# Attention, a mixture of experts and a dense layer in one kernel: GpSimd instead of SyncE issues some loads between the experts

## The chip, the cores and the metric

The kernel runs on one core of a Trainium2 chip. The metric is the device time of one execution, in microseconds (us); a kernel's time is the median of its runs. Queues: SP is SyncE's instruction stream, POOL is GpSimd's, and both issue DMAs; PE is TensorE, DVE VectorE, ACT ScalarE.

## What is computed

```
x = causal_attention(q, k, v)            # 4 x 12 heads, 448 positions, 64 wide: 1792 tokens x 768
e = argmax(x @ w_gate)                   # one of 8 experts for each token
y = gate * relu(x[e] @ w1[e]) @ w2[e]    # w1: 8 x 768 x 1024, w2: 8 x 1024 x 768
h = y @ w_in                             # 768 x 2048
out = (h - tanh(h)) @ w_out              # 2048 x 768
```

Inputs and output are float32. The kernel splits each float32 operand into a high and a low float16 part and multiplies three of the four combinations.

## The kernel before, in words

There are three stages: attention with the routing (0 to about 235 us in the profile), the experts (to about 535 us), and the last stage with the dense layer (to the end). The change touches the experts, which are run one after the other.

**A slot** (`slot`, L872) is 128 tokens of one expert. Expert e has one first slot, which always runs, and then as many further slots as its token count asks for; these stand in nested branches (`extra`, L945: `tc.If` at L949, taken or skipped on a count that all engines hold in a register). In the profiled run the experts 1 to 6 take 2, 3, 1, 2, 1 and 5 slots. PE does in a slot 144 matmuls of the first product (`mm1_f`, L164), then 12 transposes of token rows for a later slot (`planes_T`, L151), then 48 matmuls of the second product in two halves (`mm2_k`, L176), in the first slot with 12 more transposes between the halves. ACT and DVE take the first product out of PSUM with the relu (`slot_relu`, L171 and L172; tiles hh and hl), and PE's second product waits for these.

**Raw loads and pieces.** The weights come from DRAM as float32 into two buffers, raw1 for w1 and raw2 for w2 (the profile calls both raw), 14 pieces in all: six of w1 (512 KB each) and eight of w2 (384 KB). While the first slot of expert e runs, ACT writes the high part of each piece of expert e+1 (L115) and DVE the low part (L123, in `pieces`), and behind that the freed place is loaded with the piece of expert e+2 (`load_raw`, L107). The slot calls `fill_lo` at four places, z = 0 to 3, with 1, 4, 4 and 5 pieces (`PLAN`, L1031). The calls z = 0 to 2 stand before the slot's result is stored (`ys_d`, L923), and the one with the last five pieces, all of w2, behind that store. All 14 loads are issued by SP, in this order, and each waits for DVE's low part of its piece.

**Other traffic.** Each further slot also converts two or three units of the dense layer's weights (`conv_fill`, L1001): a unit of 1 MB is loaded into one of the buffers cu (`conv_load`, L990, SP), DVE and ACT turn it into float16 planes (L980 to L986, L115, L123; tiles cc and co), and the planes are stored (`conv_store`, L1007, SP). A unit's load waits for DVE to have read the unit before it in that buffer. GpSimd fetches token rows by index (`slot_rows`, L861, tiles xg and xg_n), each behind the transposes that read the rows before, and does some elementwise work. In expert 6's first slot, behind its store, SP loads the first six row blocks of the last stage (`prep0`, L1071; 384 KB each) from ys_d into the raw buffers, which are free by then; they wait for all stores to ys_d so far.

**Branches.** A branch that is skipped has a path of its own, in which the semaphores are brought to where the taken path would leave them. On SP these paths wait for the DMAs that SP has in flight on the named semaphores.

Of the kernel before, what the change touches and what calls it, by code (L numbers as in the profile page):

```python
# [19 lines left out]
AX = mybir.AxisListType  # L20
PSUM = bass.MemoryType.PSUM
SP = mybir.EngineType.SP

B, H, S, D = 4, 12, 448, 64
CP, NCH = 112, 4
# [30 lines left out]
GS = [sum(GB[:i]) for i in range(len(GB))]  # L56
# [3 lines left out]
def build(ctx: ExitStack, tc: tile.TileContext, kq0, kq, v, wg, wo, w1, w2, wf, out):  # L60
    nc = tc.nc
# [27 lines left out]
    flg = cst.tile([1, 5], I32, name="flg")  # L89
# [5 lines left out]
    raw1 = raw_p.tile([128, KD, F1], F32, name="raw1")  # L95
    raw2 = raw_p.tile([128, KF1, DM], F32, name="raw2")
# [6 lines left out]
    mctl = tc.manual_schedule()  # L103
    mctl.__enter__()

    def load_raw(e, x, k, n=1):
        nc.sync.dma_start(out=(raw1, raw2)[x][:, k : k + n, :], in_=(w1, w2)[x][e, :, k : k + n, :])  # L107

    def w_tiles(e, zs=(0, 1)):
        return [w16s[e % 2][z].tile((([128, 2, KD, F1]), [128, 2, KF1, DM])[z], F16, tag=f"w{z + 1}", name=f"w{z + 1}_{e}")  # L110
# [23 lines left out]
        for x, k, eh, el in plan:  # L134
            scaled(eh, w[x][:, 0, k, :], (raw1, raw2)[x][:, k, :])

    def pieces(w, plan, nxt=None, hi=True):
        if hi:
            pieces_hi(w, plan)
        for x, k, eh, el in plan:  # L140
            rest_of(el, w[x][:, 1, k, :], (raw1, raw2)[x][:, k, :], w[x][:, 0, k, :])
        if nxt is not None and nxt < E:
            for x, k, eh, el in plan:
                load_raw(nxt, x, k)

    def planes_T(rows, hi, lo, pool, tag="t", eng="a"):
        for x, dst in enumerate((hi, lo)):
# [786 lines left out]
    ystores = {}  # L934

    def after(ins, names):
        for n in names:
            tc.add_manual_dep(ins, n, mybir.DependencyInfo(mybir.DependencyClass.Sync, mybir.DependencyReason.DATA),
                              reason="reads or overwrites what these stores wrote")
# [125 lines left out]
    yq_of = lambda g, i: first["yq"][g][i] if g < 2 else G["yq"]  # L1065
    dg_of = lambda g, i: first["dg"][g][i] if g < 2 else dgs[i % 2]

    def prep0(g, i, r0=None, to=None):
        bk = GS[g] + i
        src = ys_d[bk * 128 : (bk + 1) * 128] if r0 is None else ys_d[ds(r0, 128)]  # L1070
        after(nc.sync.dma_start(out=yg_of(g, i) if to is None else to, in_=src).ins, sum(ystores.values(), []))  # L1071

    def prep_s(g, i, n):
        b0 = GS[g] + i
# [128 lines left out]
    wts = {0: wts0, 1: wts1 + w_tiles(1, (1,))}  # L1203
# [24 lines left out]
    for e in range(E):  # L1228
        if e == 0:
            slot_rows(0, 2, 1)  # L1230
            slot_rows(1, 0, "n")
        slot_rows(e, 2 + FB[e], 0)
        if e == 0:
            next(tl, None)
        if e + 1 < E:
            if e:
                wts[e + 1] = w_tiles(e + 1)

            def fill_hi(z, e=e):
                todo = PLANS[e]  # L1240
                if e:
                    pieces_hi(wts[e + 1], sum(todo, [])[CUT[z] : CUT[z + 1]])
                else:
                    pieces_hi(wts[e + 1], todo[max(z - 1, 0)] if z != 1 else [])

            def fill_lo(z, e=e):
                if e == 0 and z >= 2:
                    next(tl, None)
                pieces(wts[e + 1], PLANS[e][z], e + 2, False)
                if e == 1 and z == 3:  # L1250
                    order_b()
                if e == E - 2 and z == 3:
                    early = nc.values_load(flg[0:1, 4:5], engines=(SP,), min_val=0, max_val=128)
                    for g in range(2):
                        for i in range(GB[g]):
                            prep0(g, i, early * (GS[g] + i) if g + i else 0)

            fill = (fill_hi, fill_lo)
        else:
            wo_ = [w16s[0][z].tile([128, KF2, DM], F16, tag=tg, name=f"wo_{z}") for z, tg in enumerate(("w1", "w2"))]  # L1260
            wof = [t.rearrange("p k f -> p (k f)") for t in wo_]
            stg = [wof[0][:, z * 4096 : (z + 1) * 4096].bitcast(U32).rearrange("p (n t) -> p n t", t=2) for z in range(2)]
            stg += [wof[1][:, z * 2048 : (z + 1) * 2048] for z in range(2)]
            planes_ = [[wof[1][:, 2048 + z * row : 2048 + (z + 1) * row] for z in range(3)],
                       c3[2:4] + [wof[1][:, 6656 : 6656 + row]]]
            first["yq"] = [[t.rearrange("p (k x n) -> p k x n", k=KD, x=2) for t in ts] for ts in planes_]
            first["dg"] = [[wof[1][:, 8192 + 768 * g + 256 * z : 8448 + 768 * g + 256 * z].bitcast(BF16).rearrange(
                "p (a n) -> p a n", a=2) for z in range(3)] for g in range(2)]
            first["sc"] = [wof[1][:, 9728 + 64 * g : 9792 + 64 * g].bitcast(F32) for g in range(2)]
            second = nc.values_load(flg[0:1, 0:1], engines=(SP,), min_val=0, max_val=128)  # L1270
            remaining()
            qc = (cc, wof[0][:, 8192:10240].bitcast(U32))

            def fill(z):
                if z == 2:
                    first_hi()
                if z in (1, 2):
                    to_f32([(qc[2 - z][:, h], cu[z - 1][:, h, :]) for h in HS])
                    conv_planes(qc[2 - z], co[z - 1][:, 0], co[z - 1][:, 1], "p")
                    conv_store(z - 1, nc.values_load(flg[0:1, z + 1 : z + 2], engines=(SP,), min_val=0, max_val=NDY - 1))  # L1280
                if z == 1:
                    for q in range(2):
                        conv_load(stg[q], NDY + q, nc.gpsimd)
                    prep_max(0, 0, GB[0])
                    first_planes()
                if z == 3:
                    prep_max(1, 0, GB[1])

            qhl = [[y[:, (10 + q) * 1024 : (11 + q) * 1024] for y in wof] for q in range(2)]

            def last_f32(q):
                to_f32([(qc[q][:, h], stg[q][:, h, :]) for h in HS])

            def last_planes(q):
                for z in range(2):
                    for h in HS:
                        c = qc[q][:, h].bitcast(F32)
                        scaled("a", qhl[q][0][:, h], c) if z == 0 else rest_of("p", qhl[q][1][:, h], c, qhl[q][0][:, h])

            def last_fill(z):  # L1300
                if z == 1:
                    last_f32(0)
                    first_rest()
                if z == 2:
                    last_planes(0)

        slot(e, FB[e], wts[e], f"n{e % 2}", fill,
             ((1, (FB[e] + 1) % 2),) + ((("n", f"n{(e + 1) % 2}"),) if e + 1 < E else ()),
             [lambda j=j: slot_rows(*j) for j in ((e + 1, 1, 1), (e + 2, 0, "n")) if j[0] < E], late=e + 1 == E, mid=lambda: counts(e))
        if e == 0:  # L1310
            for _ in tl:
                pass
            sctx.close()
            cv = w16ctx.enter_context(tc.tile_pool(reuse_waits="tile", name="cv", bufs=1, side="right"))
            cu = [cv.tile([128, 1024, 2], U32, name=f"cu_{z}") for z in range(2)]
            cc = cv.tile([128, 1024], U32, name="cc")
            co = [cv.tile([128, 2, 1024], F16, name=f"co_{z}") for z in range(2)]
            cuf = [t.rearrange("p n t -> p (n t)").bitcast(F16) for t in cu]
            cof = [t.rearrange("p a n -> p (a n)") for t in co]
            ccf = cc.bitcast(F32)  # L1320
            ny = KD * 384
            spare = [t[:, ny:4096].bitcast(F32) for t in cuf]
            yg1 = cof[1][:, 0 : 2 * DM].bitcast(F32)
            dgs = [cof[1][:, 1536 + 256 * z : 1792 + 256 * z].bitcast(BF16).rearrange("p (a n) -> p a n", a=2) for z in range(2)]
            rss = [cof[0][:, 768 * z : 768 * (z + 1)].bitcast(BF16).rearrange("p (a n) -> p a n", a=2) for z in range(2)]
            sc = [cof[0][:, 1536 + 64 * z : 1600 + 64 * z].bitcast(F32) for z in range(2)]
            G = {0: {"yh": cuf[0][:, 0:ny].rearrange("p (k n) -> p k n", k=KD),
                     "yl": cuf[1][:, 0:ny].rearrange("p (k n) -> p k n", k=KD), "rs": rss[0]}}
            oba = cof[1][:CP, 0 : NC_ * 128].bitcast(BF16).rearrange("p (c n) -> p c n", n=128)
            ob = ccf[:CP, 0 : 3 * NC_ * NBLK].bitcast(BF16)  # L1330
            obm = ob[:, 0 : NC_ * NBLK].rearrange("p (c n) -> p c n", c=NC_)
            obb = ob[:, NC_ * NBLK :].rearrange("p (c n z) -> p c n z", c=NC_, z=5)
            for z in range(3):
                order_a(z)
            conv_load(cu[0], 0)
        if e == E - 1:
            wi_load(nc.sync, 0)
        extra(e, 1 + FB[e], wts[e])
        if e == 0:
            conv_load(cu[1], unit_of(1, 1))  # L1340
# [200 lines left out]
```

## Time and profile before

| | |
|---|---|
| median of 3 runs | 1000.73 us (996.85 to 1002.29) |
| profiled execution | 998.19 us, of which the span of the trace is 996.5 us |
| PE busy | 956.4 us of the span |
| DVE, ACT, POOL busy | 788.6, 613.8, 471.7 us |
| DMA queue of SP / of GpSimd | 144.68 MB / 19.80 MB |

The profiled execution is 2.54 us below the median. A busy time of an engine is a sum over its instructions; an idle time before an instruction is put down to what came last of what it waited for. DMA-issuing instructions on SP are shown where SP issues them (SPq); on POOL a DMA's span is the time that GpSimd works on issuing it. "To landing" is from issue to the last byte.

### The profile page before, as it was taken

To read this page: it belongs to the slowest core of one execution; us is meant where nothing else is said; L and a number is where in the kernel's file an instruction comes from. 1 tells how busy PE (TensorE), PEld (TensorE's weight loads), DVE (VectorE), ACT (ScalarE), POOL (GpSimd) and SP (SyncE) were. 2 spreads that over 40 slices of the span, in tenths; PEclk is the share of its full clock that TensorE was granted. 3 is DMA by queue.
4 is the path that set the end of the run, shared out by engine and by line. 5 is a ranking of instruction groups with operands and counts; after the bars stand their busy time and mean duration, and the time that the engine had idled before them with its cause. 6 is when DMAs were issued, how large, how long until landed. Compare 5 with 4: busy or idle time off the path is not lost. (4 is left out here: it accounts for less than half of the span.)

```text
span 996.5 us, 24098 instructions
## 1 busy us (share of the span) xinstructions
PE 956.4 (96%) x9177; PEld 714.8 (72%) x9177; DVE 788.6 (79%) x1740; ACT 613.8 (62%) x1176; POOL 471.7 (47%) x536
## 2 busy tenths in 40 slices
PE   5999999998999999998999899999999999999996
PEld 4998989986787878787686556666666666677764
DVE  7878888978879598797888999887988788786630
ACT  5898988763645484753356896656565556565530
POOL 7668887872211020202246797555544434443321
PEclk9999999999999999999999999999999999999999
DMA  9787786576799999979876430010000000000000
GB/s 253 213 234 212 217 230 181 164 258 239 274 399 335 345 344 344 345 266 327 305 289 233 171 152 17 32 33 17 24 25 32 17 25 17 9 17 17 16 25 24
DMA packets 59703, 166.36 MB, mean 167 GB/s; under 512 B 7904, under 2 KB 21856, under 8 KB 56480
## 3 DMA queue, kind: packets, MB, share of 16 engines
q1 hardware_dynamic: 54992, 144.68, 43.1%
q0 software_dynamic: 4560, 19.80, 5.8%
q8 instruction: 80, 1.31, 0.5%
q14 instruction: 71, 0.58, 0.2%
HBM read 122.21 MB, written 29.62 MB: 152 GB/s over the span
## 5 line engine op out<-in xcount | busy, mean ns | idle before, releaser
L1430 PE MATMUL fo<-wo,g 128*128 128x384 f16 x1344 | 228.2, 326 | 0.0
L1379 PEld LDWEIGHTS <-raw 128*128 128x128 f16 x1440 | 140.7, 98 | 85.2 <-issue 6.9
L1430 PEld LDWEIGHTS <-g 128*128 128x128 f16 x1344 | 131.2, 98 | 83.8
L1389 POOL TENSOR_TENSOR V<-cu,cc 128x384 f32<-128x384 f32 (+1 forms) x80 | 79.2, 990 | 185.6 <-ACT cu L1388 184.5
L164 PEld LDWEIGHTS <-w 128*128 128x128 f16 x2592 | 145.8, 98 | 7.7 <-issue 6.6
L1379 PE MATMUL fh<-cu,raw 128*128 128x384 f16 (+1 forms) x864 | 131.8, 308 | 3.3 <-DVE cc L1387 3.3
L378 ACT ACTIVATE P<-s,nb 112x112 f32<-112x112 f32 (+1 forms) x192 | 91.4, 509 | 23.6 <-DVE nb L370 21.6
L123 DVE SCALAR_TENSOR_TENSOR w<-raw,w 128x768 f16<-128x768 f32 (+1 forms) x99 | 99.7, 1067 | 0.2 <-ACT w L115 0.2
L861 POOL DMA_INDIRECT xg<-xs_d,idx x22 | 26.9, 1221 | 150.8 <-PEq L949 29.2
L1388 ACT ACTIVATE cu<-cc 128x384 f32<-128x384 f32 (+1 forms) x80 | 40.0, 500 | 92.5 <-DVE cc L1387 92.5
L115 ACT ACTIVATE w<-raw 128x768 f16<-128x768 f32 (+2 forms) x106 | 90.0, 909 | 9.8 <-DMA raw<-w 5.5
L370 DVE CUSTOM_DVE_ANT_0 s<-s,maskw 112x112 f32<-112x112 f32 (+1 forms) x192 | 86.1, 455 | 9.5 <-PE s L364 4.6
L1387 DVE TENSOR_TENSOR cc<-fh,co 128x384 f32<-128x384 f32 (+1 forms) x80 | 42.0, 525 | 63.2 <-PE fh L1379 50.2
L1392 POOL TENSOR_TENSOR X<-cc,X 128x384 f32<-128x384 f32 (+1 forms) x80 | 88.2, 1102 | 4.1 <-ACT X L1391 0.5
L427 PE MATMUL o<-v,PT 112*112 112x65 f32 x576 | 83.8, 269 | 0.0
L1399 DVE SCALAR_TENSOR_TENSOR V<-cu,V 128x384 f32<-128x384 f32 (+1 forms) x80 | 82.2, 1028 | 0.2
L1407 DVE TENSOR_TENSOR V<-V,co 128x384 f32<-128x384 f32 (+1 forms) x64 | 78.3, 1224 | 0.0
L1408 ACT ACTIVATE g<-V 128x384 f16<-128x384 f32 (+1 forms) x80 | 40.0, 500 | 46.4 <-DVE V L1407 46.3
L1379 PE MATMUL fh<-yh,raw 128*128 128x384 f16 x384 | 67.6, 326 | 0.7 <-DVE cc L1387 0.7
L397 PE MATMUL t<-ident,P 112*112 112x112 f32 x480 | 68.0, 265 | 0.0
L427 PEld LDWEIGHTS o<-v,PT 112*112 112x112 f32 x576 | 67.8, 177 | 0.0
L363 PE MATMUL s<-kh,qa 128*112 128x112 f16 (+1 forms) x192 | 53.8, 302 | 11.4 <-POOL qa L298 7.3
(677 smaller groups left out, 2093.9 us busy)
## 6 DMA issues: line engine op xcount, KB each, us to landing
raw<-w SPq DMA_DIRECT2D x48, 512.0 KB, 7.3
raw<-w SPq DMA_DIRECT2D x64, 384.0 KB, 9.4
cu<-wf SPq DMA_DIRECT2D x22, 1024.0 KB, 8.2
wb_d<-co SPq DMA_DIRECT2D x22, 512.0 KB, 8.1
raw<-kq SPq DMA_DIRECT2D x11, 896.0 KB, 6.9
raw<-wb_d SPq DMA_DIRECT2D x8, 768.0 KB, 4.6
raw<-v SPq DMA_DIRECT2D x12, 448.0 KB, 7.5
xs_d<-xq SPq DMA_DIRECT2D x24, 224.0 KB, 2.5
```

What stands on the lines that cost most here:

```text
L115: nc.scalar.activation(out=out, in_=in_, func=AF.Copy, scale=WS)
L123: nc.vector.scalar_tensor_tensor(out=out, in0=in_, scalar=WS, in1=hi, op0=ALU.mult, op1=ALU.subtract)
L164: nc.tensor.matmul(out=ph[:, (f % 4) * 128 : (f % 4 + 1) * 128], lhsT=w[0][:, ww, k, f * 128 : (f + 1) * 128], rhs=xTs[tag][:, xx, k, :], ...
L370: nc.vector.tensor_tensor_reduce(out=d["s", m][:, z, :], in0=d["s", m][:, z, :], in1=maskw[:, S - n : S], scale=-0.125, scalar=3.0e38, op0 ...
L378: nc.scalar.activation(out=d["P"][:, j, OFF[i] : OFF[i] + n], in_=d["s", m][:, z, :], func=AF.Exp, bias=d["nb"][:, 2 * i + j : 2 * i + j + ...
L427: nc.tensor.matmul(out=po[:, i, :], lhsT=d["PT"][:, PT_AT[g], o : o + CP], rhs=d["t"][3][:, hl, j, :], start=(j == 0), stop=(j == i))
L1379: nc.tensor.matmul(out=ph[:, 0:nt], lhsT=wi[ww][:, f // 4, k, f % 4 * 128 : (f % 4 + 1) * 128], rhs=yy[:, k, 0:nt], start=(q == 0), stop=( ...
L1389: nc.gpsimd.tensor_tensor(out=d["V"], in0=d["U"], in1=d["h"], op=ALU.mult)
L1392: nc.gpsimd.tensor_tensor(out=d["X"], in0=d["h"], in1=d["X"], op=ALU.subtract)
L1399: nc.vector.scalar_tensor_tensor(out=d["V"], in0=d[f"S{z}"], scalar=QD[z - 1], in1=d["V"], op0=ALU.add, op1=ALU.mult)
L1407: nc.vector.tensor_tensor(out=d["V"], in0=d["V"], in1=rs_y(g, nt), op=ALU.mult)
L1430: nc.tensor.matmul(out=po[:, 0:384], lhsT=t[:, x, k, i * 128 : (i + 1) * 128], rhs=wo_[ww][:, k, z * 384 : (z + 1) * 384], start=(k == 0 a ...
```

## The change

`load_raw` and `prep0` get a parameter for the issuing engine. From expert 1 on, the loads behind the last five pieces (z = 3) are issued by GpSimd; so are the six row loads in expert 6's first slot, with the register that holds their stride (`early`), which is now loaded on POOL. What is loaded, where to, and what each load waits for on DVE stay.

```diff
-    def load_raw(e, x, k, n=1):
-        nc.sync.dma_start(out=(raw1, raw2)[x][:, k : k + n, :], in_=(w1, w2)[x][e, :, k : k + n, :])
+    def load_raw(e, x, k, n=1, eng=nc.sync):
+        eng.dma_start(out=(raw1, raw2)[x][:, k : k + n, :], in_=(w1, w2)[x][e, :, k : k + n, :])
...
-    def pieces(w, plan, nxt=None, hi=True):
+    def pieces(w, plan, nxt=None, hi=True, eng=nc.sync):
...
-                load_raw(nxt, x, k)
+                load_raw(nxt, x, k, 1, eng)
...
-    def prep0(g, i, r0=None, to=None):
+    def prep0(g, i, r0=None, to=None, eng=nc.sync):
...
-        after(nc.sync.dma_start(out=yg_of(g, i) if to is None else to, in_=src).ins, sum(ystores.values(), []))
+        after(eng.dma_start(out=yg_of(g, i) if to is None else to, in_=src).ins, sum(ystores.values(), []))
...
-                pieces(wts[e + 1], PLANS[e][z], e + 2, False)
+                pieces(wts[e + 1], PLANS[e][z], e + 2, False, nc.gpsimd if e and z == 3 else nc.sync)
...
-                    early = nc.values_load(flg[0:1, 4:5], engines=(SP,), min_val=0, max_val=128)
+                    early = nc.values_load(flg[0:1, 4:5], engines=(POOL,), min_val=0, max_val=128)
...
-                            prep0(g, i, early * (GS[g] + i) if g + i else 0)
+                            prep0(g, i, early * (GS[g] + i) if g + i else 0, None, nc.gpsimd)
```

In the order of instructions only SP and POOL differ. On SP behind expert 5's first slot (the store of its result, then the branch to its further slots), before:

```order
L923 ISA
L923 DMA ys_d<-yo_I-14133_14134 128x768
L107 DMA raw_90<-w 128x768 x5
L949 COMPARE_AND_BRANCH
L944 REGISTER_ALU
L1537 BRANCH_PREFETCH_HINT
```

and now:

```order
L924 ISA
L924 DMA ys_d<-yo_I-14133_14134 128x768
L950 COMPARE_AND_BRANCH
L945 REGISTER_ALU
L1538 BRANCH_PREFETCH_HINT
```

The five loads have left SP; they stand on POOL, in expert 5's first slot behind the fetch of xg_n. With the semaphores that each row waits for (DMASW are those of GpSimd's own DMAs, used in turn), before:

```order
L861 DMA xg_n<-xs_d,idx 128x1536 [waits DMASW6_49,PE_49]
L949 COMPARE_AND_BRANCH
L944 REGISTER_ALU
L1537 BRANCH_PREFETCH_HINT
L861 DMA xg_4588<-xs_d,idx 128x1536 [waits DMASW2_49,PE_49]
```

now, with the fetches at expert 6's beginning as the last two rows:

```order
L862 DMA xg_n<-xs_d,idx 128x1536 [waits DMASW0_49,PE_49]
L108 DMA raw_90<-w 128x768 [waits DMASW1_49,DVE_49]
L108 DMA raw_90<-w 128x768 [waits DMASW2_49,DVE_49]
L108 DMA raw_90<-w 128x768 [waits DVE_49] x3
L950 COMPARE_AND_BRANCH
...
L862 DMA xg_4588<-xs_d,idx 128x1536 [waits DMASW6_49,DMASW1_49,DMASW7_49,DMASW0_49,PE_49]
L862 DMA xg_4589<-xs_d,idx 128x1536 [waits DMASW2_49,PE_49]
```

All of the next expert's fetches now stand behind the five loads, and the first of them waits for the semaphore DMASW1, which the first of the five uses.

On SP behind expert 6's first slot, before (of the six row loads three are left out here):

```order
L923 DMA ys_d<-yo_I-16037_16038 128x768
L1253 TENSOR_LOAD flg
L1253 ISA x2
L1071 DMA raw_89<-ys_d 128x768
L1071 ISA
L1071 DMA raw_89<-ys_d 128x768
...
L1071 DMA raw_90<-ys_d 128x768
L949 COMPARE_AND_BRANCH
...
L990 DMA cu_4987<-wf 128x2048
```

and now:

```order
L924 DMA ys_d<-yo_I-16037_16038 128x768
L950 COMPARE_AND_BRANCH
L945 REGISTER_ALU
L1538 BRANCH_PREFETCH_HINT
L1017 TENSOR_LOAD xtab
L1017 ISA x2
L991 ISA
L991 DMA cu_4987<-wf 128x2048
```

SP comes from the store straight to the unit's load; the six row loads stand on POOL, ahead of the fetch of token rows in expert 6's first further slot.

## Rows read from the trace of the kernel before

**Rows 1.** The head of the page.

```profile
span 996.5 us, 24098 instructions
```

**Rows 2.** Windows: stretch, length, busy PE, PEld, DVE, ACT, POOL, clock, DMA share, GB/s.

```profile
250.00:430.00 180.00, 177.09 (x2189) 142.28 (x2188) 146.56 (x212) 104.95 (x149) 28.23 (x22) 1.00 0.93 342
450.00:530.00 80.00, 75.37 (x899) 59.16 (x897) 67.07 (x122) 31.50 (x58) 28.23 (x30) 1.00 0.84 298
```

**Rows 3.** Waits of PE, 250 to 530 us: us in total, times, longest.

```profile
PE py_I-16959_16960 L176 <- ACT hh_I-16750_16751 L171: 2.2, 1, 2.2
PE py_I-17308_17309 L176 <- ACT hh_I-17100_17101 L171: 0.9, 1, 0.9
PE py_I-16221_16222 L176 <- ACT hh_I-16033_16034 L171: 0.8, 1, 0.8
PE py_I-16959_16960 L176 <- DVE hl_I-16752_16753 L172: 0.2, 1, 0.2
```

**Rows 4.** Timeline of SP, 395 to 440 us: start, length, instruction.

```profile
395.96 0.59 SPq L1007 DMA_DIRECT2D wb_d<-co  x1
408.94 6.61 SPq L107 DMA_DIRECT2D raw<-w  x9
417.97 0.36 SPq L923 DMA_DIRECT2D ys_d<-yo_I-14133_14134  x1
419.17 5.75 SPq L107 DMA_DIRECT2D raw<-w  x5
435.07 0.35 SPq L923 DMA_DIRECT2D ys_d<-yo_I-16037_16038  x1
438.32 3.54 SPq L1071 DMA_DIRECT2D raw<-ys_d  x6
442.94 0.33 SPq L990 DMA_DIRECT2D cu<-wf  x1
```

**Rows 5.** Waits of SP, 395 to 412 us.

```profile
SPq L949 <- SPq L949: 11.6, 5, 5.1
```

**Rows 6.** Timeline of DVE, 400 to 460 us; in brackets idle time before, and what ended it.

```profile
406.11 0.55 DVE L119 TENSOR_SCALAR w<-raw 128x768 f16<-128x768 f32 x1
...
407.05 8.16 DVE L123 SCALAR_TENSOR_TENSOR w<-raw,w 128x1024 f16<-128x1024 f32 x9
439.76 1.28 DVE L986 SCALAR_TENSOR_TENSOR cc<-cu,cc 128x512 uint32<-128x512 uint32 x2
451.06 0.76 DVE L980 TENSOR_SCALAR cc<-cu 128x512 uint32<-128x512 uint32 x2 [4.16 <-DMA cu<-wf]
```

**Rows 7.** Timeline of ACT, 415 to 456 us.

```profile
417.85 1.06 ACT L115 ACTIVATE w<-raw 128x1024 f16<-128x1024 f32 x1 [1.87 <-DMA raw<-w]
453.71 1.24 ACT L115 ACTIVATE co<-cc 128x512 f16<-128x512 f32 x2 [7.15 <-DVE cc L986]
```

**Rows 8.** Timeline of POOL, 400 to 440 us.

```profile
405.35 1.66 POOL L861 DMA_INDIRECT xg_n<-xs_d,idx  x1 [3.63 <-PE pt_I-14416_14417 L151]
409.34 1.48 POOL L861 DMA_INDIRECT xg<-xs_d,idx  x1 [2.33 <-PEq L949]
437.09 0.94 POOL L861 DMA_INDIRECT xg<-xs_d,idx  x1 [17.88 <-PE pt_I-16567_16568 L151]
```

**Rows 9.** GpSimd's issues, by line: least, median and greatest ns; then their landing.

```profile
L990 POOL DMA_DIRECT2D wo<-wf x2: 577/604/631, 515.9 to 516.5; - x2
L861 POOL DMA_INDIRECT xg<-xs_d,idx x22: 940/942/3551, 234.9 to 510.0; - x22
DMA to landing us min/median/max: 3.6/7.1/11.0
```

**Rows 10.** DMAs cu<-wf, SP's line L990: least, median and greatest us to landing.

```profile
DMA to landing us min/median/max: 5.5/8.2/12.1
```

**Rows 11.** Timeline of PE: the transposes of fetched rows in expert 6's first two further slots.

```profile
435.98 0.50 PE L151 MATMUL pt_I-16558_16559<-identh,xg 128*128 128x128 f16 x6
452.49 0.50 PE L151 MATMUL pt_I-16908_16909<-identh,xg 128*128 128x128 f16 x6
```

More of the change, by code (lines that the diff above doesn't have):

```diff
@@ L22 @@
 SP = mybir.EngineType.SP
+POOL = mybir.EngineType.Pool
 B, H, S, D = 4, 12, 448, 64
```

## The prediction

> **What bounds the kernel now.** I start from the head of the page for the span, 996.5 us [rows 1], and then ask what PE waits for where the change acts, between 250 and 530 us. The windows say that PE is busy for 177.09 of the 180 us up to 430, and for 75.37 of the 80 us from 450 on [rows 2]: this stage is PE's, and whatever any queue does earlier or later is worth only what it takes from PE's idle 2.9 and 4.6 us, or adds to them. The waits of PE name the parts that a load can reach [rows 3]: 0.8 us in expert 6's first slot and 2.2 + 0.2 us in its third (its second further slot), both for the relu of ACT and DVE (hh, hl), and 0.9 us in its fourth. A part of the rest is the fetch of code at branches, which no load changes.
>
> Next, what makes the relu late. In expert 6's first slot ACT, which works in order, stands for 1.87 us before a high part, for a raw load [rows 7]; the relu comes behind it. In the third slot ACT stands for 7.15 us behind DVE's conversion [rows 7], and DVE for 4.16 us, until 451.06, for a unit's load [rows 6].
>
> Then SP's timeline, for why those loads are late [rows 4]. The unit's load is issued at 442.94. DVE had read the unit before it by 441.04 (439.76 + 1.28) [rows 6]; in between SP was busy with the six row loads, 438.32 to 441.86, which wait for the store of 435.07 to land. And behind expert 4's last store (395.96) SP issues nothing until 408.94: 11.6 us of that are waits of the skipped branches for SP's own DMAs [rows 5]. Then come nine raw loads, the slot's store at 417.97, and the last five from 419.17 on. DVE was done with all their pieces at 415.21 (407.05 + 8.16) [rows 6].
>
> **The change, part by part.** The sum is made against the profiled execution, 998.19 us, which lies 2.54 below the median of 1000.73.
>
> *Twenty-five raw loads leave SP* (five each in experts 1 to 5). On POOL they no longer stand behind the store, so each can go when DVE has finished its piece: in expert 5 the last at about 415 instead of 424. Each is needed one first slot later, so being earlier is worth nothing by itself. What counts is that SP has fewer DMAs to wait for in the skipped branches and that less is queued ahead of its own, so that the raw load which ACT misses by 1.87 us comes earlier. With that PE's 0.8 us goes. I take -0.8; bounds 0 (the transfers share the same engines, and only their order changes) and -1.0 (the 0.2 us of DVE behind it as well).
>
> *The six row loads leave SP.* The unit's load goes at about 441.1 instead of 442.94: 1.8 us earlier. That alone leaves 4.16 - 1.8 = 2.4 us of DVE's wait and 2.4 - 1.8 = 0.6 us of PE's. Besides, the load no longer queues behind 2.4 MB of rows in SP's queue. Before, it landed 8.1 us after its issue; the least of the 22 such loads is 5.5 [rows 10], so up to 2.6 us more. I take -2.2, near the upper bound of -2.4 (the whole stall), because the rows and the unit now sit in two queues and the unit no longer has to let all rows pass; the lower bound is 0. The Trainium skill, DMA: Bandwidth & Descriptors, section "Issuing engines are not separate DMA queues", says that DMAs issued by several engines interleave on the same 16 DMA engines and that this saves only the issuing time. By that rule the term would be the 1.8 us alone.
>
> *Expert 6's later slots* keep their waits, which come from units issued as soon as DVE lets them: 0, with bounds of 0 and -1.3 (0.9, and some 0.4 for DVE's parts).
>
> *What GpSimd has to do for it.* The nearest row is the only plain DMA it issues today, 577 to 631 ns [rows 9]; a fetch by index takes 942 ns in the middle, 3.55 us once [rows 9]. I take 0.6 us. 25 x 0.6 + 6 x 0.6 = 18.6 us of POOL, of which nothing lies on the path by itself: in this stage POOL is busy for 28 of 180 us [rows 2]. What counts is who stands behind them:
> - The five loads: behind them is the next expert's first fetch, which by the order now also waits for the first of the five to land. In expert 5 that is at about 411.6 + 8.2 = 420 (0.9 us of DVE for each piece, 8.2 us to landing as a unit's load has it [rows 10]) instead of 409.34 [rows 8]. The rows then land at about 420.6 + 7.1 = 428 [rows 9], by the greatest landing at 432. PE transposes them at 435.98 [rows 11]. Cost 0, cover 4 to 8 us; in expert 3, the other case without a further slot, the same distance.
> - The six row loads: POOL waits as SP did until 438.32, then 6 x 0.7 us (0.6 and the register work between) to 442.5. The fetch behind them leaves at 442.5 instead of 437.09 [rows 8] and lands 7.1 us later at 449.6, at worst 11.0 later at 453.5. PE transposes these rows at 452.49 [rows 11]. Cost 0; bounds 0 and +1.0 (453.5 - 452.49), or +2.8 if the loads take 1 us each and the landing is the worst one. This is the thinnest cover of all.
>
> Sum: -0.8 - 2.2 + 0 + 0 = **-3.0 us**: 995.2 for the profiled execution, and from the median 1000.73 - 3.0 = **997.7 us**. What PE gains in this stage is passed on to the end, since in the last stage PE and DVE follow on each other without a fixed date.
>
> **Rivals.**
> 1. *Nothing to see* (within 1 us of before, some 1000.7). The unit's load and the rows move the same bytes over the same engines, so the unit may land at 451 all the same, and what the first slot gains is lost again at the third slot's transposes. For it: DMA runs at 0.93 of its share up to 430 and 0.84 after [rows 2]. Against it: the queue is idle just before 438, so the unit's load is held back by issue and order there, not by a backlog.
> 2. *Slower: GpSimd's issuing becomes the wait.* Place: the fetch behind the six row loads. It has to leave by 452.49 - 7.1 = 445.4, so the loads may take (445.4 - 438.3) / 6 = 1.2 us each. A fetch of xg_n took 1.66 us at 405.35 instead of 0.94 [rows 8, 9]; one fetch took 3.55. With 1.66 each: 438.3 + 10.0 + 7.1 = 455.4, 2.9 us after 452.49, which replaces the 2.4 us of before: about 1000.4 with the first slot's gain. With 3.55 each: 438.3 + 21.3 + 7.1 = 466.7, a stall of 14.2 instead of 2.4, so 1000.7 - 0.8 + 11.8 = 1011.7. It decides from about 2.5 us each on. The Trainium skill, SBUF — State Buffer, section "SBUF: two separate sides", says that GpSimd cannot write a DMA's descriptors while DVE runs an instruction in a mode that takes the port they share. The trace agrees for the issue at 405.35, during which DVE scales a piece (L119, 406.11 [rows 6]). Against the rival: at the moved loads DVE mostly runs other lines (L123, L983), and the middle of the fetches beside those is 942 ns [rows 9]; only two short L980 fall on the six.
> 3. *All waits for loads go* (0.8 + 0.2 + 2.2 + 0.2 + 0.9 + 0.4 = 4.7 us): 996.0. For it: DVE and ACT come through the third slot earlier, and each later slot inherits that. Against: the 0.9 us hangs on a unit that is issued without delay already.
> 4. *The loads do not come earlier*, if POOL is held up by its fetches ahead of them: then only the second term is left, 998.5. The order speaks against it: the fetch before the five is done in the middle of the slot, at 407.0 in expert 5 [rows 8].
>
> **How the numbers follow.** Chances: forecast, with rival 4 as its weaker form, 0.52; rival 1 0.25; rival 2 0.10; rival 3 0.13. A measurement tells 0.5% (5 us: below 995.7 or above 1005.7) from no change. The forecast lies 2.0 above that line and the three runs of before lie 5.4 apart, so a sixth of its chance falls below (0.09); rival 3 lies at 996.0, so nearly half does (0.06); with 0.02 for the rest, faster is 0.17. Slower is rival 2 where its loads take over 2.5 us (0.07) and 0.02 of stray: 0.09. Same is 0.74. The range reaches down to rival 3 less 3 us of scatter, 993.0, and up to no change plus 2.8, half of the runs' scatter or the cost of a late fetch: 1003.5.
>
> **What would show it.** Right: on SP the unit's load of expert 6's second slot at 441 to 442 and no loads behind the stores; DVE's wait of 4.16 us under 2 us; the wait of PE for hh in the third slot under 0.5 us, that in the first slot gone; on POOL the five loads before the store, 0.6 us each; the fetch behind the six at about 443, landed before PE's transposes. Wrong: a wait of PE for xg; loads on POOL of over 1 us; DVE's wait unchanged though the unit's load left earlier (rival 1); a longer stretch elsewhere, such as PE's idle time from 530 us on, which I take as untouched.

## The result, and the profile after

The changed kernel took 1009.60 us (median of 6 runs, 1007.53 to 1011.85) beside 1000.62 us of the kernel before on the same chip (6 runs): ratio 1.0089, 95% interval 1.0070 to 1.0109. It is slower by 9 us; I had forecast 3 us less. A second group of runs gave 1.0068 (1.0043 to 1.0093).

The profiled execution (1009.23 us) is 11.0 us longer than that of before [rows 1]. Windows of the changed kernel, columns as in [rows 2]; the last two are new:

```profile
250.00:430.00 180.00, 176.99 (x2178) 141.69 (x2177) 143.59 (x208) 101.95 (x145) 44.15 (x47) 1.00 0.91 339
450.00:530.00 80.00, 78.15 (x981) 63.28 (x980) 64.72 (x118) 30.89 (x58) 25.70 (x28) 1.00 0.88 319
...
440.00:445.00 5.00, 2.50 (x8) 1.01 (x9) 5.00 (x9) 2.57 (x5) 1.11 (x1) 0.66 0.20 79
445.00:450.00 5.00, 5.00 (x23) 2.54 (x21) 4.91 (x9) 1.69 (x3) 3.73 (x7) 0.66 0.83 251
```

The two long stretches look no worse than before. What is new lies between them: PE's granted clock is 0.66 from 440 to 450 us. The waits of PE, 250 to 530 us, name what came ahead of it:

```profile
PE py_I-16609_16610 L177 <- ACT hh_I-16400_16401 L172: 3.1, 1, 3.1
PE py_I-16609_16610 L177 <- DVE hl_I-16402_16403 L173: 1.1, 1, 1.1
...
PE py_I-16959_16960 L177 <- ACT hh_I-16750_16751 L172: 0.6, 1, 0.6
```

The 2.2 us of [rows 3] in expert 6's third slot shrank to 0.6 and the 0.8 us of its first slot went, as forecast; but its second slot, which had no wait, got one of 3.1 + 1.1 us. The shrinking is luck: the wait behind it, DVE's for the weight unit, did not get shorter (below), PE only came to it later. A second profile of the changed kernel (run e9) has the third slot's wait in full, and the second slot's again:

```profile
PE py_I-16609_16610 L177 <- ACT hh_I-16400_16401 L172: 2.8, 1, 2.8
PE py_I-16959_16960 L177 <- ACT hh_I-16750_16751 L172: 2.4, 1, 2.4
PE py_I-16609_16610 L177 <- DVE hl_I-16402_16403 L173: 1.4, 1, 1.4
```

The timeline of SP in the first profile puts dates to it (lines answer to [rows 4]):

```profile
399.07 0.58 SPq L1008 DMA_DIRECT2D wb_d<-co  x1
413.04 5.47 SPq L108 DMA_DIRECT2D raw<-w  x9
419.36 0.36 SPq L924 DMA_DIRECT2D ys_d<-yo_I-14133_14134  x1
440.92 0.35 SPq L924 DMA_DIRECT2D ys_d<-yo_I-16037_16038  x1
447.35 0.36 SPq L991 DMA_DIRECT2D cu<-wf  x1
...
456.84 0.37 SPq L924 DMA_DIRECT2D ys_d<-yo_I-16404_16405  x1
```

Each store marks the end of a slot. Against before, expert 5's store is 1.4 us late (419.36 for 417.97), the first one of expert 6 5.9 (440.92 for 435.07), the second 8.2 (456.84 for 448.64). The first of these two waits for ACT, which copies the result out, and not for PE: PE began the second slot at 429.44, 1.5 us late (427.94 before), and loses in it the 4.2 us of waits and some 2.9 us of slower matmuls behind them. The later slots win 2.5 back: expert 7's last store is 5.7 late. The other 5.3 of the 11.0 us lie behind it.

Why ACT is late in the first slot is seen on its own timeline (rows of 410 to 440 us; before, its longest waits for raw loads were 1.87 [rows 7] and 1.95 us):

```profile
417.13 1.06 ACT L116 ACTIVATE w<-raw 128x1024 f16<-128x1024 f32 x1 [4.15 <-DMA raw<-w]
...
426.70 1.06 ACT L116 ACTIVATE w<-raw 128x1024 f16<-128x1024 f32 x1 [1.86 <-SPq L950]
429.57 1.06 ACT L116 ACTIVATE w<-raw 128x1024 f16<-128x1024 f32 x1 [1.82 <-SPq L950]
...
434.68 0.84 ACT L116 ACTIVATE w<-raw 128x768 f16<-128x768 f32 x1 [2.58 <-SPq L950]
...
436.74 3.77 ACT L116 ACTIVATE w<-raw 128x768 f16<-128x768 f32 x5
```

ACT waits for the nine pieces that SP loads, up to 434.68; the five of GpSimd's loads (the last line) it takes without a wait. The waits put down to SP's queue (SPq) end with landings too: the last of the nine was issued at 418.11 and landed 16.5 us later, at 434.66, and ACT took it at 434.68. ACT had little to spare: before, it had idled 1.3 us ahead of the second slot's relu. POOL itself did what was forecast (lines answer to [rows 8]; the last fetch is the one behind the six row loads):

```profile
414.44 0.57 POOL L108 DMA_DIRECT2D raw<-w  x1 [5.03 <-DVE w L124]
...
423.34 2.01 POOL L862 DMA_INDIRECT xg<-xs_d,idx  x1 [4.89 <-DMA raw<-w]
...
443.89 3.84 POOL L1072 DMA_DIRECT2D raw<-ys_d  x6 [16.29 <-DVE hl_I-16402_16403 L173]
448.03 1.01 POOL L862 DMA_INDIRECT xg<-xs_d,idx  x1 [0.30 <-issue]
```

And DVE's wait for the weight unit, 4.16 us in [rows 6], is still there:

```profile
446.02 1.30 DVE L987 SCALAR_TENSOR_TENSOR cc<-cu,cc 128x512 uint32<-128x512 uint32 x2
...
458.28 0.76 DVE L981 TENSOR_SCALAR cc<-cu 128x512 uint32<-128x512 uint32 x2 [4.88 <-DMA cu<-wf]
```

The unit's load now left at 447.35, at once when DVE had read the unit before it (446.02 + 1.30); before it had left 1.9 us after that. But from issue to DVE's start it took 10.9 us, where it had taken 8.1 (442.94 to 451.06). In the four other profiles with the row loads on GpSimd it took 9.0 (e2), 11.2 (e5), 9.9 (e6) and 11.7 us (e9).

### The profile page after: what moved, and what is told of

The parts are those of the page before. It is cut to its first block, busy times and chain, and to the rows that moved or that the text cites. A ratio compares the mean times of both kernels' runs of the same rounds, so it can differ in the third digit from the quotient of the medians.

```text
span 1007.5 us, 24102 instructions
## 1 busy us (share of the span) xinstructions
PE 961.0 (95%) x9177; PEld 716.3 (71%) x9177; DVE 789.1 (78%) x1740; ACT 613.9 (61%) x1176; POOL 491.0 (49%) x567
## 5 line engine op out<-in xcount | busy, mean ns | idle before, releaser
L116 ACT ACTIVATE w<-raw 128x768 f16<-128x768 f32 (+2 forms) x106 | 90.1, 908 | 21.0 <-SPq L950 11.8
```

Of the source, the lines that this page charges most:

```text
L116: nc.scalar.activation(out=out, in_=in_, func=AF.Copy, scale=WS)
```

## The experiments

Seventeen runs followed; e5, e9 and e17 repeat a kernel. "Nine" are the raw loads of a slot that are needed first, "five" the last ones. Ratios are to the kernel before on the same chip.

| run | on GpSimd, other edits | median us (runs) | before | ratio, 95% interval |
|---|---|---|---|---|
| e1 | five | 1002.97 (10) | 1000.78 | 1.0024, 1.0011 to 1.0038 |
| e2 | rows | 1005.54 (5) | 1000.78 | 1.0057, 1.0040 to 1.0074 |
| e3 | five of experts 1, 2, 4; rows | 1002.02 (10) | 1000.78 | 1.0016, 0.9996 to 1.0035 |
| e4 | five of expert 5 | 1006.10 (5) | 1000.78 | 1.0054, 1.0026 to 1.0083 |
| e5 | as e2 | 1000.18 (10) | 999.14 | 1.0021, 0.9999 to 1.0043 |
| e6 | rows; fetch ahead of them | 1000.16 (10) | 999.14 | 1.0013, 0.9991 to 1.0035 |
| e7 | none; five left out | 992.06 (9) | 999.14 | 0.9919, 0.9894 to 0.9944 |
| e8 | five, behind the nine's landing | 1013.84 (4) | 999.14 | 1.0142, 1.0100 to 1.0185 |
| e9 | the change again | 1008.08 (7) | 1002.09 | 1.0068, 1.0043 to 1.0093 |
| e10 | none; rows left out | 996.37 (4) | 1002.09 | 0.9938, 0.9920 to 0.9956 |
| e11 | nine and five | 995.26 (10) | 1002.09 | 0.9962, 0.9924 to 1.0000 |
| e12 | none; three rows later | 998.56 (6) | 1002.09 | 0.9965, 0.9944 to 0.9985 |
| e13 | nine | 997.74 (10) | 998.73 | 0.9978, 0.9955 to 1.0000 |
| e14 | nine and five; three rows later | 996.82 (12) | 998.73 | 0.9994, 0.9960 to 1.0028 |
| e15 | nine, five and rows | 998.9 (1) | 998.73 | one execution |
| e16 | nine; three rows later | 997.43 (10) | 1001.58 | 0.9966, 0.9950 to 0.9982 |
| e17 | as e13 | 997.48 (7) | 1001.58 | 0.9956, 0.9941 to 0.9972 |

**The halves alone (e1, e2) and parts of the first (e3, e4).** e1 is the change without its lines in `prep0`, e2 without the one in `fill_lo`:

```
-                pieces(wts[e + 1], PLANS[e][z], e + 2, False, nc.gpsimd if e and z == 3 else nc.sync)
+                pieces(wts[e + 1], PLANS[e][z], e + 2, False, nc.sync)
```

In e3 the condition is `e in (1, 2, 4) and z == 3`, with the row loads on GpSimd; in e4 `e == 5 and z == 3`, without them.

> The 25 raw loads on GpSimd, the six row loads back on SyncE. Theory A (the five raw loads of an expert without further slots run beside SyncE's nine and make those late, so that in expert 6's first slot ScalarE's high parts and with them the relu of the second slot come late): the whole loss before 530 us is here, a wait of PE for hh of some 4 us at the second slot of expert 6 and a lower granted clock behind it, and a time of 1007 to 1012. Rival B (the row loads on GpSimd cost the time, through the fetch behind them): within 2 us of before, 999 to 1002. Rival C (both halves cost): about 1004.

> The six row loads on GpSimd, all raw loads back on SyncE. Theory A: no loss; the unit's load leaves at 441 instead of 443 and PE's 2.4 us in expert 6's third slot shrink, so 998 to 1000. Rival B: 1005 to 1010, with PE or the second slot waiting for fetched rows. If the wait of DVE for the unit stays at 4 us although its load leaves earlier, the prediction's second term was wrong by itself.

> As the change, but the five raw loads of experts 3 and 5, which have no further slot, are issued by SyncE again. Theory A: the loss is gone, 998 to 1001, no wait of PE for hh in expert 6's second slot. Rival B: still 1005 or more. Rival D (any raw load on GpSimd costs a little, through sharing of the DMA engines in every slot): a loss of about 3/5 of the whole, 1004 to 1007.

> As before the change, but the five raw loads of expert 5 alone are issued by GpSimd. Theory A: most of the loss, 1004 to 1010, with ScalarE's high parts in expert 6's first slot late by up to 4 us and PE's wait at its second slot. Rival D: 1 to 2 us of loss. Rival E (the loss comes from SyncE's nine loads leaving later, because the skipped branches behind experts 3 and 4 hold it longer): no loss, 999 to 1002, since experts 3 and 4 are as before.

Each half alone costs something: +0.24%, and +0.57% or, in e5, +0.21% with an interval that touches no change. e1 shows the first half without the second. There SP issued expert 5's nine loads at 409.54, hardly later than before (408.94), and still PE waited 3.0 + 1.4 us in expert 6's second slot. The DMA views, 402 to 417 us, of before and then of e1 (issuing queue, count, size of one, median us to landing) say why:

```profile
raw<-w SPq DMA_DIRECT2D x6, 512.0 KB, 9.2
raw<-w SPq DMA_DIRECT2D x3, 384.0 KB, 11.5
```

```profile
raw<-w SPq DMA_DIRECT2D x6, 512.0 KB, 6.4
raw<-w POOLq DMA_DIRECT2D x5, 384.0 KB, 9.1
raw<-w SPq DMA_DIRECT2D x3, 384.0 KB, 15.9
```

The last three of the nine took 15.9 us where the same three had taken 11.5, and 11.3 in e7, which has no five beside them; the five, which ACT takes up only at 433 us, took 9.1. The first six of the nine, most of them issued ahead of the five, did not suffer (6.4 us for 9.2). Two queues brought the less urgent bytes in ahead of the last of the urgent ones. e4 is inconclusive: in its profile SP was late where its program is still that of before (expert 4's five loads at 393.06, before at 383.23). So executions differ in how far SP falls behind. e3's time lies within the scatter of e1 and e5; but its profile, with expert 5's five on SP, has no wait of PE in expert 6's second slot, as those of e2, e5 and e6 have none.

**What the rows lose (e5, e6).** e6 puts the fetch of expert 6's fourth slot ahead of the row loads, into the tile `xg_n`, which has no further use by then, from where the later transposes read them:

```
                 if e == E - 2 and z == 3:
+                    slot_rows(e, 3, "n")
                     early = nc.values_load(flg[0:1, 4:5], engines=(POOL,), min_val=0, max_val=128)
```

> The same kernel as the run with the row loads alone on GpSimd, for a second profile: the profiled execution there was the fastest of five (998.83 us, median 1005.54), so what the typical one loses was not seen. Theory 'fetch': the row gather of expert 6's fourth slot, behind six row loads on GpSimd and sharing the DMA engines with them, lands late, PE waits for it in the third slot (1.2 us in the profile there) and the granted clock falls behind it; then the stores of expert 6 from the third slot on (448.64 before) are 3 us or more late. Theory 'last stage': the stores up to 532.89 are within 1.5 us of before and 3 us or more are lost behind 540, at DVE's first work on the rows. Time: 1003 to 1007 by both.

> Row loads on GpSimd as in the run with them alone, raw loads on SP, but the gather of expert 6's fourth slot goes into the tile that the second transposition has just freed and stands ahead of the six row loads on GpSimd, where it stood behind them. Theory 'fetch': no wait of PE for gathered rows, the stall at the third slot and the fall of the clock behind it are gone, 997 to 1001 us. Theory 'last stage': the gather costs nothing that counts, and the time stays at 1004 to 1007 us.

Waits of PE, 400 to 470 us, in e5 and then in e6:

```profile
PE py_I-16221_16222 L177 <- ACT hh_I-16033_16034 L172: 2.8, 1, 2.8
PE py_I-16959_16960 L177 <- ACT hh_I-16750_16751 L172: 2.5, 1, 2.5
PE pt_I-16908_16909 L152 <- DMA xg<-xs_d,idx: 0.6, 1, 0.6
```

```profile
PE py_I-16959_16960 L177 <- ACT hh_I-16750_16751 L172: 2.6, 1, 2.6
PE py_I-16221_16222 L177 <- ACT hh_I-16033_16034 L172: 2.2, 1, 2.2
```

The wait for the fetched rows (0.6 us; 1.2 in e2) is gone in e6, and the ratio hardly moved, its interval overlapping that of e5: the fetch is real and small. What stays in both is the 2.5 us in the third slot that moving the row loads was to remove (1.4 in e2, whose profile is that of its fastest run). In the windows of five microseconds from 455 to 465 us the granted clock is down to 0.70 in e5 and 0.82 in e6, where before has 1.00.

**Bytes and order (e7, e8).** e7 passes `E` for `e + 2` where z is 3; in e8 `load_raw` on GpSimd carries `after(ld, nine[-1:])`, `nine` being the names of SP's loads.

> The kernel before with the last five raw loads of each slot from expert 1 on left out altogether (neither SP nor GpSimd issues them; the conversions run on what the tile holds from an expert before, so the output is another). Theory 'sharing' (the five on GpSimd's queue take half of the DMA engines from the nine that are needed first, and SP, which drains its own loads in skipped branches, gets later with each expert): with no five there is nothing to share, expert 5's nine loads leave SP before 409 us, ACT's waits for them in expert 6's first slot are under 2 us in all, time 995 to 999 us. Theory 'SP's drain' (with the five gone from SP's queue the skipped branches drain the nine, and ACT is released only by SP's own instructions there): ACT's waits released by SP's queue stay at 8 us or more as with the change, PE stalls in expert 6's first or second slot, 1001 to 1006 us.

> Row loads on SP; the five raw loads on GpSimd, but each waits until the ninth load of SP has landed, so that the two queues do not move them at the same time (GpSimd stands still until then, with the row gathers behind it). Theory 'sharing': the nine land as before, ACT's waits in expert 6's first slot shrink to the 5 us of before or less, time 998 to 1002 us unless the gathers behind come late (PE would then wait for gathered rows at about 436 us). Theory 'SP's drain': SP's waits in the skipped branches and ACT's waits behind them are as with the five on GpSimd without the wait (1003 us there), 1002 to 1006 us.

Without the five, PE waited for a relu in no slot for more than 0.2 us, from 250 to 530 us, and the kernel gained 7 to 8 us: that is what the five cost where they stand in the kernel before. It is not the price of their bytes alone, since SP also came to the nine earlier (404.81). SP's program is that of e1, yet the ACT waits that end with SP's queue came to 0.2 us, where e1 has 9.1: they are not made by SP's branches alone, but by bytes in the way. e8 lost 14 us, elsewhere: PE waited 6.0, 2.5 and 1.5 us for fetched rows, which stood behind the waiting loads on GpSimd. It tells nothing on the order of landing, but shows what a blocked GpSimd costs.

**The change again (e9) and both kinds of load (e15).**

> The changed kernel once more, beside the others of this group. If its loss is the raw loads' (2 to 3 us alone) and the row loads' (1 to 5 us alone) and nothing of its own, 1003 to 1008 us; 1008 to 1011 us, as first measured, if the two together cost more than their sum. A second profile shows whether what the first one had in the last stage (one wait of 4.0 us of TensorE for DVE, where the kernel before has seven of at most 1.2) belongs to the change or to one execution.

> All fourteen raw loads and all six row loads on GpSimd. If DVE's gap of 3.3 to 3.5 us in the last stage goes with both kinds of loads being on GpSimd, it is there again, 3 us or more, with TensorE's wait of about 4 us behind it; if it goes with the lateness of the kernel before it or with SP's part of the raw loads, it is under 1 us. Time 996 to 1006 us.

The last stage of the first profile (PE and DVE, 555 to 561 us) and then PE's and DVE's waits of e9, 540 to 565 us:

```profile
561.13 4.70 PE L1380 MATMUL fh<-cu,raw 128*128 128x384 f16 x18 [3.95 <-DVE cc L1388]
...
558.65 0.56 DVE L1400 SCALAR_TENSOR_TENSOR V<-cu,V 128x384 f32<-128x384 f32 x1 [3.30 <-issue]
```

```profile
PE fh L1380 <- DVE cc L1388: 4.1, 1, 4.1
DVE V L1400 <- issue: 3.5, 1, 3.5
```

Both profiles of the change have a gap of 3.3 to 3.5 us on DVE at the same instruction, with no wait to be seen, and PE's wait of 4 us behind it. In every other profile PE's longest wait of this kind is 2.1 us or less, in before's 1.2. In both, an 8 KB transfer of the queue that the profile calls "instruction" falls into the gap, 1.5 and 1.7 us behind its start. In 16 of the other 17 profiles one of that size comes 1.9 to 3.4 us ahead of the same place, and DVE goes on at once; in e7 none comes near it, and DVE goes on too. So code that DVE gets late would fit, but the profile does not tell whose code a transfer brings, and the cause is not shown. e15 has both kinds of load on GpSimd, and in its one execution the longest wait is 1.1 us, so the combination alone need not make it. Why the change has it stays open.

**The bytes of the rows (e10, e12).** e10 drops the loop of `prep0` calls; e12 moves half of it:

```
-                    for g in range(2):
-                        for i in range(GB[g]):
-                            prep0(g, i, early * (GS[g] + i) if g + i else 0)
+                    for i in range(GB[0]):
+                        prep0(0, i, early * (GS[0] + i) if i else 0)
+                    first["early"] = early
...
+            for i in range(GB[1]):
+                prep0(1, i, first["early"] * (GS[1] + i))
             remaining()
```

> The kernel before with the six row loads of expert 6's first slot left out (the last stage works on what lies in the tile, so the output is another): what their bytes cost where they stand, whoever issues them. Theory 'sharing': the weight unit that DVE waits for in expert 6's second slot (4.16 us before, 4.88 with the change) has the DMA engines to itself and lands in time, DVE's wait is under 1.5 us, TensorE's stall in the third slot (2.4 us) is gone, 996 to 998.5 us. Theory 'place in the queue' (the unit is late only because SP issues it behind the six): the same gain, but then the change, which took the six out of SP's way, should have had it too, and had not. If the time stays within 1 us of before, the six cost nothing there and the row loads' own part of the loss has another cause.

> The kernel before with three of the six row loads (those of the second group, first read at about 521 us) issued by SP at the start of expert 7, about 503 us, where they had stood behind the other three at 440 us. Theory 'sharing': 1.2 MB fewer in front of and beside the weight unit in expert 6's second slot, at 400 GB/s some 3 us; DVE's wait for the unit falls from 4.2 to 1 to 2 us, TensorE's stall in the third slot from 2.4 to under 1 us, 998 to 1000 us where the kernel before has 1000. If the bytes are not what the unit waits for, no change; if the three land after 521 us, DVE waits for them in expert 7 and the time is 1002 us or more.

DVE's waits for units, 430 to 470 us, in e10 and then in e12 (before, 6.0 us at two places, 4.16 of them at [rows 6]):

```profile
DVE cc L981 <- DMA cu<-wf: 0.6, 1, 0.6
```

```profile
DVE cc L981 <- DMA cu<-wf: 3.3, 2, 2.2
```

Without the rows the waits fall to 0.6 us and PE's stall in the third slot is gone. With half of them later, the one wait is 1.15 us at 449.07, another of 2.2 comes later, PE's stall is gone and the kernel gains 0.35%; the three that stay are SP's. e2 and e10 set the two causes apart, since SP issues the unit's load at the same time in both. Issue and first use of the unit, in e2 (rows on GpSimd) and then in e10 (no rows):

```profile
440.65 0.36 SPq L991 DMA_DIRECT2D cu<-wf  x1
449.66 0.77 DVE L981 TENSOR_SCALAR cc<-cu 128x512 uint32<-128x512 uint32 x2 [3.18 <-DMA cu<-wf]
```

```profile
440.60 0.36 SPq L991 DMA_DIRECT2D cu<-wf  x1
446.34 0.76 DVE L981 TENSOR_SCALAR cc<-cu 128x512 uint32<-128x512 uint32 x2
```

With the rows beside it the unit is there 9.0 us after its issue, without them within 5.7, and DVE does not wait. It is the rows' bytes beside the unit that count, not who issues them.

**The nine instead of the five (e11, e13, e17), and both gains together (e14, e16).** e11 has `nc.gpsimd if e else nc.sync` in `fill_lo`; e13 and e17, the mirror of the change:

```
-                pieces(wts[e + 1], PLANS[e][z], e + 2, False)
+                pieces(wts[e + 1], PLANS[e][z], e + 2, False, nc.gpsimd if e and z < 3 else nc.sync)
```

e14 and e16 add e12's edit to e11 and e13.

> Row loads on SP as before; all fourteen raw loads of a slot from expert 1 on go to GpSimd, so that they are again in one queue in the order in which they are needed. Theory 'sharing': the five no longer run beside the nine, ACT's waits for raw pieces in expert 6's first slot that end with SP's queue (9 to 12 us with the five alone on GpSimd) vanish, and the time is not above the 1003 us of the five alone: 997 to 1002 us. Against it: the row gathers stand behind the raw loads on GpSimd, which wait for DVE piece by piece; if they come late as in the run in which GpSimd waited for the ninth load (1013.8 us), TensorE waits for gathered rows and the time is 1004 to 1012 us.

> Row loads on SP; the nine raw loads that are needed first go to GpSimd from expert 1 on, the last five stay on SP. Theory 'two queues': the five again move beside the nine where they overlap; ACT's waits for the nine in expert 6's first slot stay at 8 us or more, 1000 to 1004 us. Theory 'SP late': GpSimd issues each of the nine as DVE frees its piece, without SP's wait in the skipped branches, the nine land early whatever runs beside them, and the time is like that with all fourteen on GpSimd, 994 to 998 us. The row gathers behind the nine on GpSimd can be late as they were there (3.5 us of TensorE in expert 6's second slot).

> The kernel with the nine raw loads on GpSimd and the last five on SP once more, with more rounds. If SP's lateness at the nine is what the executions of the kernel before differ by and what the change makes worse, ratio 0.995 to 0.999 with an interval below 1, and the runs lie closer together than those of before (4 us from lowest to highest, where before has 6 to 10). If the first result was chance, 1.000.

> The two edits that each came out below the kernel before, together: all fourteen raw loads on GpSimd (995.3 us alone) and three of the six row loads moved to the start of expert 7 on SP (998.6 us alone, 0.35% under before). If they remove different stalls (late raw pieces up to expert 6's first slot; the late weight unit behind it), 992 to 995 us. If the gather that was late with all fourteen on GpSimd sets the end, no better than 995 us.

> The nine raw loads that are needed first on GpSimd, the last five on SP (997.7 us alone, ratio 0.9978), and three of the six row loads at the start of expert 7 on SP (0.9965 alone). In the profile of the first of these TensorE had no wait over 0.7 us between 250 and 530 us and the clock stayed whole, so that little is left for the second edit there: 994 to 998 us, ratio 0.994 to 0.998. At 0.998 or above the two remove the same stall.

The DMA view of e13, 400 to 442 us (the first of the nine left ahead of it), and POOL's first and last of expert 5's nine loads:

```profile
raw<-w POOLq DMA_DIRECT2D x5, 512.0 KB, 7.2
...
raw<-w SPq DMA_DIRECT2D x5, 384.0 KB, 12.4
raw<-w POOLq DMA_DIRECT2D x3, 384.0 KB, 9.7
```

```profile
399.09 0.57 POOL L108 DMA_DIRECT2D raw<-w  x1 [5.96 <-ACT w L116]
...
411.34 0.54 POOL L108 DMA_DIRECT2D raw<-w  x1 [0.32 <-DVE w L124]
```

The nine left from 399.09 on, as soon as a piece was free, while SP, still in its skipped branches, had come to them only at 408.94 before and 413.04 with the change. Here they landed in 7 to 10 us in the middle, and the five, for which nobody waits yet, in 12. The last of the nine was in at 421.5, where the change has 434.66. About half of the difference is earlier issue (411.34 for 418.11), the rest a shorter way (10.2 us for 16.5). All of the nine left ahead of the five here, which explains that as well as their queue would; these runs do not separate the two. Over 250 to 430 us PE was busy for 178.22 us (177.09 before [rows 2]), and it waited for no relu for more than 0.2 us up to 530 (in e17's profile, of its slowest run, for two, 0.9 us each). e17's interval, 0.9941 to 0.9972, excludes no change: the mirror of the change is 0.4% faster than the kernel before. The second edit adds nothing to it (e16, 0.9966). e11 has a lower median, though not a lower ratio than e17, and two of its ten runs took 1006.8 and 1008.7 us and three of e14's twelve over 1008; its profile shows PE waiting 3.5 us for fetched rows behind fourteen loads on GpSimd. e13 and e17 stay between 995.6 and 999.6 in all 17 runs. The kernel of e13 and e17 is the version that beats both, the one before and the change.

## Why the prediction was wrong

**What bounds the stage.** The reading "this stage is PE's" held on average and missed the margin. The DMA share of 0.93 [rows 2] was taken as a point for a rival, though it decides what an order costs: without 25 loads the kernel is 7 to 8 us faster (e7), and with the nine of each slot issued earlier, and all loads in place, 0.4% (e17).

**The raw loads, -0.8.** This step failed, in sign. It named the lower bound's reason ("the transfers share the same engines, and only their order changes") and took the other end. Two things of it were wrong. Less queued ahead of SP's own loads was no help, since the five then ran beside them: e1's last three landed after 15.9 us instead of 11.5. And SP did not get through the skipped branches sooner: its waits there from 395 us up to the nine loads were 12.6 us with the change, 11.6 before [rows 5]. Nor was its lateness needed for the loss: in e9 it came to the nine at 409.20, and PE lost 2.8 + 1.4 us all the same. Measured: +0.24% alone, some 2.4 us. The 0.8 us of PE did go, and 4.2 us came one slot later; rival 1 had named a loss further on, but at the wrong place (the third slot). The bounds, 0 and -1.0, excluded a loss with no row that did so.

**The row loads, -2.2.** The size failed. The 1.9 us of issue were gained, and 2.8 us lost in landing, so that DVE's wait was 4.88 us; e2 and e5 put the half at +0.57% and +0.21%. That PE's wait in the third slot shrank in the first profile was luck, as e9's 2.4 us show. The sentence "the unit no longer has to let all rows pass" was the wrong one: in two queues it passes beside them, 9.0 us for 5.7 without them (e2, e10). Rival 1, at 0.25, had this mechanism: the same bytes over the same engines. The Trainium skill, DMA: Bandwidth & Descriptors, section "Issuing engines are not separate DMA queues", which I had weighed and set aside, says that such DMAs interleave on the same 16 engines and that only issuing time is saved. The traces agree, and add that the landing can become worse by more than the issue gains.

**GpSimd's issuing, 0.** Right in price: 0.54 to 0.64 us each, 3.84 for the six, with none of the 1.2 us that rival 2 needed. One reading is not borne out: the fetch at 405.35 was put down to DVE's L119, but the one at 409.34 took 1.48 us beside L123 alone [rows 6, 8], and the 942 ns are the middle of all 22 fetches, not of those beside L123. The place of the risk was right all the same, "the thinnest cover": with the rows alone PE waited 0.6 to 1.2 us for the fetch. In the change itself PE was late anyway and did not wait.

**"What PE gains is passed on to the end."** The loss was passed on, and more: 5.3 of the profile's 11.0 us lie behind the last store, in which the step took PE as untouched. Some 4 us are the gap on DVE with PE's wait; behind it 18 matmuls took 4.70 us, 261 ns each, where the eight ahead of the gap took 1.46 us, 183 each (granted clock 0.66 from 560 to 565 us).

**The chances.** A slower result was given 0.09, all of it to GpSimd's issuing. A rival in which the loads moved beside others delay those was not among them, although both DMA rows that it needs, the share of 0.93 and nine loads issued at 408.94 with five pieces free by 415.21, stood in the text.

## What to carry to other kernels

Where the DMA share is near 1 (0.93 here), one queue is a priority list: its order says whose bytes come first. Moving the later loads of that list to another engine's queue does not relieve the earlier ones, it puts the later ones beside them. If a second queue is to be used, give it the loads that are needed first, where its engine is free to issue them as early as their buffers allow; and before costing an issue, look up what else is in flight when it lands.

## What was not expected of the hardware

- After PE's waits of 3.1 and 1.1 us the granted clock was 0.66 over the ten microseconds from 440 on, a mix of the two levels of 2.4 and 1.2 GHz; in e13, without such waits, it was 1.00 there. So a stall of 4.2 us cost PE some 2.9 us more in slower matmuls: the 48 of the second product took 11.8 us (441.44 to 453.24), 1.1 of them the second wait, where they had taken 7.8.
- Executions of one kernel differ in how late SP gets to the nine loads of expert 5: 408.94 in before's profile, 412.66 and 413.64 in e6's and e5's, whose program is the same up to there. With the nine on GpSimd the runs of before, 995.0 to 1004.2 us, become 995.6 to 999.6.
- The gap of 3.3 to 3.5 us on DVE in the last stage, twice at the same instruction, has no cause that these runs show; in both, a transfer of the queue "instruction" comes later than in the profiles without the gap.
